# A GELU feed-forward kernel: the order of loads and transposes in its first six microseconds

## The chip, the core and the metric

The kernel runs on one core of one Trainium2 chip. The metric is the device time of one execution, in microseconds, as the median of several runs. Times inside an execution come from one profiled execution and are counted from the start of its span.

## What is computed

```python
B, S, D, F = 1, 2048, 448, 1792          # all bfloat16
def reference(x, w1, b1, w2, b2):
    h = jnp.einsum("bsd,df->bsf", x, w1) + b1
    h = _gelu(h)                          # tanh approximation
    return jnp.einsum("bsf,fd->bsd", h, w2) + b2
```

x is 2048 tokens by 448, w1 448 by 1792, w2 1792 by 448.

## The kernel before

Layer 1 computes the hidden activations transposed: an output tile has 128 hidden features on the partitions and 512 tokens (a chunk) along the free side. There are 4 chunks and 14 feature tiles, so 56 tiles, in the list `order`. Eight PSUM banks hold tiles in turn. ScalarE (ACT) applies Gelu with the bias b1 to each finished tile and writes it to `g_sb`. Layer 2 (`l2`) then takes 128 tokens at a time over the 14 feature tiles; VectorE (DVE) adds b2 and the SyncE queue (SP) stores the rows.

The contraction of layer 1 has length 448, cut into four slots of rows of w1 (`KROW`): three of 128 rows, and the remaining 64 rows held twice, so that two half-height passes can share the array. TensorE's work in layer 1 is the list `steps`: each step is two matmuls (passes), for tiles i and i+1. The first 23 steps are written out by hand in `OPEN`; a fourth number in an entry picks one half (256 tokens) of chunk 0. In the text, step 0 is `(0, 2, 0, 0)`: tiles 0 and 1, slot 0, first half of the tokens. Step 1 is the same for tiles 2 and 3. Steps 2 and 3 are these with the second half of the tokens; steps 4 and 5 are slot 0 of tiles 4 to 7, all 512 tokens; steps 6 and 7 slot 1 of tiles 0 to 3.

The matmuls need x with the contraction on the partitions. For chunks 1 to 3 DMA transposes do that (`load_xT`). Chunk 0 is loaded as it is, in two halves, into `xn_sb` (semaphores `sem_xn[0]` and `sem_xn[1]`), and TensorE turns it: `turn_x(n)` multiplies 128 by 128 blocks with an identity matrix that GpSimd (POOL) makes, and a cast brings the result from PSUM into `xT_sb`. The work is cut into six parts, each with the engine of its cast ("d" VectorE, "a" ScalarE) and its pairs (half, slot):

```python
    XPARTS = [
        ("d", [(0, 0)]), ("a", [(0, 1)]), ("a", [(0, 2), (0, 3)]),
        ("d", [(1, 0)]), ("d", [(1, 1)]), ("a", [(1, 2), (1, 3)]),
    ]
    XBANK = [0, 2, 4, 5, 6, 7]
```

Each pair is two transposes, so the six parts are 2, 2, 4, 2, 2 and 4. `XBANK` is the PSUM bank that a part's result stands in until it is cast; the tile of that number can't be begun before. Parts 0 to `XLATE` - 1 are turned before step 0, the others just before step `EARLY` = 2. Before the first transpose TensorE runs constant matmuls (`NWARM` of `WN` columns) whose results nobody reads. `opening_waits` makes a step wait for the pieces of w1 and the casts that its passes read: step 0 for w1's first piece (slot 0, tiles 0 to 3) and part 0; step 2 for part 3.

Loads are issued from two queues. SP (`sync_work`) issues x's two halves, then w1's pieces of slots 0 and 1 (`load_w1p`, four pieces of 128 KB in all, of which one is on ACT's queue), the rest of w1, the DMA transposes, w2 and b2. ACT (`scalar_work`) issues b1 and w1's first piece, then loads its function table and makes its casts.

Of the kernel before, what the change touches and what calls it, by code (L numbers as in the profile page):

```python
# [7 lines left out]
BF16 = mybir.dt.bfloat16  # L8
# [3 lines left out]
def bass_standalone__dense_activation_gelu__prompt_kernel(  # L12
# [10 lines left out]
    P = 128  # L23
# [18 lines left out]
    W1_PIECES = [(0, 4), (4, 8)]  # L42
# [26 lines left out]
    ]  # L69
    XBANK = [0, 2, 4, 5, 6, 7]  # L70

    XLATE = 5
    EARLY = 2

    SQ = 32
    NB = 8

    NWARM = 12
    WN = 256


    OCUT = 320
# [42 lines left out]
    with ExitStack() as es:  # L125
# [4 lines left out]
        xn_sb = sb("xn_sb", [P, STC, D], BF16)  # L130
# [8 lines left out]
        ps = [es.enter_context(nc.psum_tensor(f"ps_{i}", [P, SC], FP32)) for i in range(NB)]  # L139
# [9 lines left out]
        sem_xn = [S_(f"sem_xn{i}") for i in range(2)]  # L149
# [17 lines left out]
        x0_view = x2[0:SC, :].rearrange("(p t) d -> p t d", t=STC)  # L167
        out0_view = out2[0:SC, :].rearrange("(p t) d -> p t d", t=STC)

        def store(eng, n):  # L170
            j, c0, c1 = outs[n]
            to = out0_view[:, j, c0:c1] if j < STC else out2[j * P:(j + 1) * P, c0:c1]
            eng.dma_start(to, out_sb[:, j, c0:c1]).then_inc(sem_od, 16)

        def x_part(n, parts):
            h, k = parts[0]
            to = xT_sb[:, k:k + len(parts), 2 * h * P:2 * (h + 1) * P]
            src = ps[XBANK[n]][:, 0:2 * P * len(parts)]
            return to, src.rearrange("p (k t) -> p k t", k=len(parts))

        def load_w1p(eng, k, i):
            a, b = W1_PIECES[i]
            r = KROW[k]
            with nc.allow_non_contiguous_dma(reason="w1 column pieces"):
                eng.dma_start(
                    w1_sb[:, k, a * P:b * P], w1[r:r + P, a * P:b * P]
                ).then_inc(sem_w1p[k][i], 16)

        def load_w1(eng):
            with nc.allow_non_contiguous_dma(reason="w1 column pieces"):  # L190
                for k in (3, 2):
                    n, r = ROWS[k], KROW[k]
                    eng.dma_start(w1_sb[0:n, k, 0:WCUT], w1[r:r + n, 0:WCUT]).then_inc(sem_w1[k], 16)
                eng.dma_start(w1_sb[:, 3, WCUT:F], w1[KROW[3]:D, WCUT:F]).then_inc(sem_w13, 16)
                eng.dma_start(
                    w1_sb[:, 0:2, WCUT:F], w1[0:2 * P, WCUT:F].rearrange("(k p) f -> p k f", p=P)
                ).then_inc(sem_w1r, 16)
                eng.dma_start(
                    w1_sb[0:HALF, 2, WCUT:F], w1[KROW[2]:KROW[2] + HALF, WCUT:F]
                ).then_inc(sem_w1r, 16)  # L200

        def load_w2(eng, i):
            a, b = W2_PIECES[i]
            eng.dma_start(
                w2_sb[:, a:b, :], w2[a * P:b * P, :].rearrange("(ft p) d -> p ft d", p=P)
            ).then_inc(sem_w2[i], 16)

        def load_xT(eng, c):
            for k, d0 in enumerate(KROW):
                eng.dma_start(  # L210
                    xT_sb[:, k, c * SC:(c + 1) * SC],
                    x2[c * SC:(c + 1) * SC, d0:d0 + P],
                    transpose=True,
                ).then_inc(sem_x[c], 16)

        def sync_work(sp):
            sp.dma_start(xn_sb[:, 0:2, :], x0_view[:, 0:2, :]).then_inc(sem_xn[0], 16)
            sp.dma_start(xn_sb[:, 2:4, :], x0_view[:, 2:4, :]).then_inc(sem_xn[1], 16)
            load_w1p(sp, 0, 1)
            for i in range(len(W1_PIECES)):  # L220
                load_w1p(sp, 1, i)
            load_w1(sp)
            load_xT(sp, 1)
            for c in range(2, NSC):
                load_xT(sp, c)
            for i in range(len(W2_PIECES)):
                load_w2(sp, i)
            sp.dma_start(b2_bc[:, :], b2.partition_broadcast(P)).then_inc(sem_b2, 16)
            for n in range(len(outs) - 1):
                sp.wait_ge(sem_osb, n + 1)  # L230
                store(sp, n)
            sp.wait_ge(sem_od, 16 * len(outs))
# [10 lines left out]

        def tensor_work(pe):
            ones_w = nc.const_aps.tensor(1.0, [P, P], BF16)
            ones_x = nc.const_aps.tensor(1.0, [P, WN], BF16)
            for _i in range(NWARM):
                pe.matmul(ps[0][:, 0:WN], lhsT=ones_w, rhs=ones_x, start=True, stop=True)  # L248
            pe.wait_ge(sem_id, 2)

            def turn_x(n):
                parts = XPARTS[n][1]
                for h, k in parts:
                    if (h, k) in ((0, 0), (1, 0)):
                        pe.wait_ge(sem_xn[h], 16)
                    for t in range(2):
                        col = parts.index((h, k)) * 2 * P + t * P
                        mm = pe.matmul(  # L258
                            ps[XBANK[n]][:, col:col + P],
                            lhsT=xn_sb[:, 2 * h + t, KROW[k]:KROW[k] + P],  # L260
                            rhs=ident[:, :],
                            start=True, stop=True,
                        )
                mm.then_inc(sem_xtp, 1)
# [46 lines left out]
            def l1():  # L311
                for n, (i, h, m, tokens) in enumerate(steps):
                    if n == EARLY:
                        for x in range(XLATE, len(XPARTS)):
                            turn_x(x)
# [45 lines left out]

            for x in range(XLATE):
                turn_x(x)
# [3 lines left out]

        def scalar_work(act):
            act.dma_start(b1n_sb[0:NFT, :], b1.rearrange("(c p) -> c p", p=P)).then_inc(sem_b1n, 16)
            load_w1p(act, 0, 0)  # L370
            zero = nc.const_aps.tensor(0.0, [P, 8], FP32)
            act.activation(act_junk[:, :], zero, ACT.Gelu_apprx_tanh)  # L372
            for n, (e, parts) in enumerate(XPARTS):
                if e == "a":
                    act.wait_ge(sem_xtp, n + 1)
                    act.copy(*x_part(n, parts)).then_inc(sem_xTa, 1)  # L376
            act.wait_ge(sem_b1, 1)
            for i, (c, ft) in enumerate(order):
                act.wait_ge(sem_l1, i + 1)
                act.activation(  # L380
                    g_sb[:, ft, c * SC:(c + 1) * SC], bank("g", i)[:, :], ACT.Gelu_apprx_tanh,
                    bias=b1_f[:, ft:ft + 1], scale=1.0,
                ).then_inc(sem_g, 1)
            act.wait_ge(sem_osb, len(outs))
            store(act, len(outs) - 1)
# [26 lines left out]


        sync_work(nc.sync)
        gpsimd_work(nc.gpsimd)
        tensor_work(nc.tensor)
        scalar_work(nc.scalar)
        vector_work(nc.vector)

# [27 lines left out]
```

## Time and profile before

| | |
|---|---|
| median of 3 runs | 93.98 us (93.93 to 94.01) |
| profiled execution, its own time | 93.20 us |
| its span | 91.9 us |
| TensorE busy | 89.2 us (97%) |
| weight loads busy | 47.3 us (52%) |
| ScalarE busy | 36.6 us (40%) |
| VectorE busy | 12.8 us (14%) |
| granted TensorE clock, mean | 1.00 |
| layer 1 passes | 384 matmuls, 42.8 us |
| layer 2 | 238 matmuls, 42.6 us |
| constant matmuls | 12, 2.7 us |
| transposes of chunk 0 | 16, 1.6 us |

In the lines of the profile, PE is TensorE's matmuls and PEld its weight loads; `ps` is a PSUM bank, `xn_sb` x as loaded, `xT_sb` x turned, `wi_sb` w1, `wo_sb` w2. A line number such as L258 is that of the kernel: L248 the constant matmuls, L258 the transposes, L275 layer 1's passes, L354 layer 2, L376 the casts on ScalarE, L391 those on VectorE, L380 Gelu. A busy TensorE is not one at its peak: the matmuls are pipelined, and a short wait can be covered by the modelled end of the one before, so starts of matmuls are read rather than busy shares.

### The profile page before, as it was taken

The page shows a single profiled execution, that of the slowest core. Times are in us where ns is not written, and L with a number is a line of the kernel's source. Part 1 is how long each engine was busy: PE and PEld are TensorE (multiplying, and loading weights), DVE is VectorE, ACT ScalarE, POOL GpSimd, SP SyncE. Part 2 cuts the span into 40 slices and gives each one's busy share as a digit, 9 for nine tenths or more (in the row PEclk, how much of TensorE's full clock was granted, in tenths as well). Part 3 has the DMA queues.
Part 4 walks back from the last instruction along what each step waited for, and adds up shares of the span by engine and source line. Part 5 has one row for each costly group of instructions (what it writes and reads, how often), then busy time and mean ns, then how long its engine had stood idle before and what let it go on. Part 6 is the DMA issues. An engine that isn't in the chain of part 4 may idle for free.

```text
span 91.9 us, 1491 instructions
## 1 busy us (share of the span) xinstructions
PE 89.2 (97%) x650; PEld 47.3 (52%) x650; DVE 12.8 (14%) x27; ACT 36.6 (40%) x61; POOL 1.3 (1%) x7
## 2 busy tenths in 40 slices
PE   6999999999999999999999999999999999999991
PEld 4664445555555555555545555555555555555571
DVE  0172000000000000000000122222112222221141
ACT  2640999877977788778974000000000000000000
POOL 5000000000000000000000000000000000000000
PEclk9999999999999999999999999999999999999999
DMA  1999856445795000000000111011111100111111
GB/s 26 342 303 274 143 112 85 95 101 114 199 375 182 0 0 4 7 0 0 0 0 0 50 55 47 7 48 50 50 50 50 50 28 29 50 50 50 50 50 50
DMA packets 12594, 7.29 MB, mean 79 GB/s; under 512 B 7203, under 2 KB 12396, under 8 KB 12588
## 3 DMA queue, kind: packets, MB, share of 16 engines
q1 hardware_dynamic: 12240, 7.03, 29.1%
q10 hardware_dynamic: 316, 0.17, 0.6%
q8 instruction: 5, 0.08, 0.3%
q0 software_dynamic: 32, 0.00, 0.0%
q14 instruction: 1, 0.01, 0.0%
HBM read 3.79 MB, written 1.84 MB: 61 GB/s over the span
## 4 chain that ended last, share of the span: by engine, by line
PE 97%; DVE 0%; issue 0%
PE ps L275 46%; PE ps L354 46%; PE ps L248 3%; PE ps L258 2%; DVE out_sb L408 0%
## 5 line engine op out<-in xcount | busy, mean ns | idle before, releaser
L275 PE MATMUL ps<-xT_sb,wi_sb 64*128 64x512 bf16 (+2 forms) x384 | 42.8, 374 | 0.0
L354 PE MATMUL ps<-wo_sb,g_sb 128*128 128x448 bf16 (+2 forms) x238 | 42.6, 342 | 0.0
L380 ACT ACTIVATE g_sb<-ps,bi_f 128x512 bf16<-128x512 f32 x56 | 33.7, 694 | 9.5 <-PE ps L275 9.5
L354 PEld LDWEIGHTS ps<-wo_sb,g_sb 128*128 128x128 bf16 x238 | 22.7, 98 | 20.2 <-issue 0.4
L275 PEld LDWEIGHTS ps<-xT_sb,wi_sb 64*128 64x128 bf16 (+1 forms) x384 | 21.8, 94 | 20.4 <-issue 0.7
L408 DVE TENSOR_TENSOR out_sb<-ps,bo_bc 128x448 bf16<-128x448 f32 (+2 forms) x17 | 10.2, 597 | 71.2 <-PE ps L354 71.2
L248 PE MATMUL ps<-const-bfloat16-1.0 128*128 128x256 bf16 x12 | 2.7, 417 | 0.8 <-PEq L432 0.8
L248 PEld LDWEIGHTS ps<-const-bfloat16-1.0 128*128 128x128 bf16 x12 | 1.6, 143 | 1.4 <-issue 0.8
L372 ACT ACT_TABLE_LOAD x1 | 1.3, 1283 | 1.8 <-issue 1.8
L376 ACT CAST xT_sb<-ps 128x512 bf16<-128x512 f32 (+1 forms) x3 | 1.5, 514 | 1.3 <-PE ps L258 1.3
L391 DVE CAST xT_sb<-ps 128x256 bf16<-128x256 f32 x3 | 1.2, 422 | 4.2 <-PE ps L258 4.2
L258 PE MATMUL ps<-ident,xn_sb 128*128 128x128 bf16 x16 | 1.6, 251 | 0.0
L258 PEld LDWEIGHTS ps<-ident,xn_sb 128*128 128x128 bf16 x16 | 1.3, 116 | 0.6 <-issue 0.5
L404 DVE COPY wi_sb<-wi_sb 64x512 bf16<-64x512 bf16 (+1 forms) x2 | 0.6, 286 | 2.0 <-DMA wi_sb<-in_w_dram 2.0
L396 DVE STREAM_TRANSPOSE bit_sb<-bin_sb 32x32 bf16<-32x32 bf16 x4 | 0.8, 200 | 0.1
L242 POOL DMA_DIRECT2D bin_sb<-in_w_dram x1 | 0.7, 655 | 0.2 <-issue 0.2
L237 POOL TENSOR_SCALAR_AFFINE_SELECT ident<-ident 128x128 bf16<-128x128 bf16 x1 | 0.3, 287 | 0.2 <-POOL ident L235 0.2
L372 ACT ACTIVATE act_junk<-const-float32-0.0 128x8 bf16<-128x8 f32 x1 | 0.2, 208 | 0.0
L235 POOL MEMSET ident<- 128x128 bf16 x1 | 0.2, 204 | 0.3 <-POOLq L432 0.3
L398 DVE CAST bi_f<-bit_sb 128x14 f32<-128x14 bf16 x1 | 0.2, 175 | 0.0
L432 POOL MEMSET const-float32-0.0<- 128x1 f32 x1 | 0.1, 98 | 0.2 <-issue 0.2
L432 POOL MEMSET const-bfloat16-1.0<- 128x1 bf16 x1 | 0.1, 101 | 0.0
(2 smaller groups left out, 0.2 us busy)
## 6 DMA issues: line engine op xcount, KB each, us to landing
out_dram<-out_sb SPq DMA_DIRECT2D x15, 112.0 KB, 1.7
wo_sb<-in_w_dram SPq DMA_DIRECT2D x2, 784.0 KB, 5.5
wi_sb<-in_w_dram SPq DMA_DIRECT2D x4, 128.0 KB, 3.5
xn_sb<-in_x_dram SPq DMA_DIRECT2D x2, 224.0 KB, 2.8
wi_sb<-in_w_dram SPq DMA_DIRECT2D x1, 384.0 KB, 5.1
wi_sb<-in_w_dram SPq DMA_DIRECT2D x1, 256.0 KB, 4.0
wi_sb<-in_w_dram SPq DMA_DIRECT2D x1, 192.0 KB, 4.5
xT_sb<-in_x_dram SPq DMA_TRANSPOSE x12, 3.4
```

Of the source, the lines that this page charges most:

```text
L242: pool.dma_start(b1n_sb[NFT:SQ, :], w1[0:SQ - NFT, 0:P]).then_inc(sem_b1x, 16)
L248: pe.matmul(ps[0][:, 0:WN], lhsT=ones_w, rhs=ones_x, start=True, stop=True)
L258: mm = pe.matmul(ps[XBANK[n]][:, col:col + P], lhsT=xn_sb[:, 2 * h + t, KROW[k]:KROW[k] + P], rhs=ident[:, :], start=True, stop=True,)
L275: return pe.matmul(bank("g", i)[:, t0:t1], lhsT=w1_sb[lo:hi, k, ft * P:(ft + 1) * P], rhs=xT_sb[lo:hi, k, c * SC + t0:c * SC + t1], start= ...
L354: mm = pe.matmul(bank("o", n)[:, 0:c1 - c0], lhsT=g_sb[:, ft, j * P:(j + 1) * P], rhs=w2_sb[:, ft, c0:c1], start=(ft == 0), stop=(ft == NF ...
L372: act.activation(act_junk[:, :], zero, ACT.Gelu_apprx_tanh)
L376: act.copy(*x_part(n, parts)).then_inc(sem_xTa, 1)
L380: act.activation(g_sb[:, ft, c * SC:(c + 1) * SC], bank("g", i)[:, :], ACT.Gelu_apprx_tanh, bias=b1_f[:, ft:ft + 1], scale=1.0,).then_inc( ...
L391: dve.tensor_copy(*x_part(n, parts)).then_inc(sem_xTd, 1)
L396: dve.transpose(b1t_sb[to, :], b1n_sb[:, to]).then_inc(sem_b1T, 1)
L404: dve.tensor_copy(two(HALF, 2), two(0, 3)).then_inc(sem_dup, 1)
L408: dve.tensor_tensor(out=out_sb[:, j, c0:c1], in0=bank("o", n)[:, 0:c1 - c0], in1=b2_bc[:, c0:c1], op=ALU.add,).then_inc(sem_osb, 1)
```

## The change

Three things are changed in the opening, and nothing behind it. The order of x's and w1's first loads: SP issues x's first half and then w1's first piece; x's second half goes from SP to ACT, in the place where w1's first piece was. `XLATE` goes from 5 to 3: before step 0 only the first half of x is turned (8 transposes in place of 12), and the whole second half (8 in place of 4) behind steps 0 and 1, which are four passes of 256 columns. And three constant matmuls of 128 columns follow the twelve of 256.

```diff
-    XLATE = 5
+    XLATE = 3
     EARLY = 2
...
-    NWARM = 12
-    WN = 256
+    WARM = [256] * 12 + [128] * 3
...
         def sync_work(sp):
             sp.dma_start(xn_sb[:, 0:2, :], x0_view[:, 0:2, :]).then_inc(sem_xn[0], 16)
-            sp.dma_start(xn_sb[:, 2:4, :], x0_view[:, 2:4, :]).then_inc(sem_xn[1], 16)
-            load_w1p(sp, 0, 1)
+            for i in range(len(W1_PIECES)):
+                load_w1p(sp, 0, i)
             for i in range(len(W1_PIECES)):
                 load_w1p(sp, 1, i)
...
         def tensor_work(pe):
             ones_w = nc.const_aps.tensor(1.0, [P, P], BF16)
-            ones_x = nc.const_aps.tensor(1.0, [P, WN], BF16)
-            for _i in range(NWARM):
-                pe.matmul(ps[0][:, 0:WN], lhsT=ones_w, rhs=ones_x, start=True, stop=True)
+            for n in WARM:
+                ones_x = nc.const_aps.tensor(1.0, [P, n], BF16)
+                pe.matmul(ps[0][:, 0:n], lhsT=ones_w, rhs=ones_x, start=True, stop=True)
             pe.wait_ge(sem_id, 2)
...
             act.dma_start(b1n_sb[0:NFT, :], b1.rearrange("(c p) -> c p", p=P)).then_inc(sem_b1n, 16)
-            load_w1p(act, 0, 0)
+            act.dma_start(xn_sb[:, 2:4, :], x0_view[:, 2:4, :]).then_inc(sem_xn[1], 16)
```

## The prediction

> **What bounds the kernel now.** I read the page first, then the chain that ended last, then the opening's timeline, then the times to landing.
>
> ```profile
> span 91.9 us, 1491 instructions
> PE 89.2 (97%) x650; PEld 47.3 (52%) x650; DVE 12.8 (14%) x27; ACT 36.6 (40%) x61; POOL 1.3 (1%) x7
> ...
> PE 97%; DVE 0%; issue 0%
> ```
>
> TensorE is the bound from 0.79 us to 90.02. The chain of waits cut into pieces (start, length, what) says where:
>
> ```profile
> 0.79 2.72 PE ps L248 x12
> ...
> 3.52 1.17 PE ps L258 x12
> 4.69 0.56 PE ps L275 x4
> 5.25 0.22 PE ps L258 x4
> 5.48 42.02 PE ps L275 x380
> 47.49 42.53 PE ps L354 x238
> ```
>
> The change touches only what stands ahead of 5.48. Behind it lie 84.5 us of matmuls. So the question is one number: when does the third step of the opening (step 2: tiles 0 and 1, second half of the tokens) start, and does the rest move with it? The timeline of the opening, in start, length, what (first matmul of a group):
>
> ```profile
> 1.20 0.42 SPq L218 DMA_DIRECT2D xn_sb<-in_x_dram  x1
> 1.44 0.36 ACTq L185 DMA_DIRECT2D wi_sb<-in_w_dram  x1
> 3.52 1.17 PE L258 MATMUL ps<-ident,xn_sb 128*128 128x128 bf16 x12
> 3.93 0.42 DVE L391 CAST xT_sb<-ps 128x256 bf16<-128x256 f32 x1 [3.93 <-PE ps L258]
> 4.62 0.76 DVE L391 CAST xT_sb<-ps 128x256 bf16<-128x256 f32 x2 [0.26 <-PE ps L258]
> 4.64 0.61 PE L275 MATMUL ps<-xT_sb,wi_sb 128*128 128x256 bf16 x4
> 5.09 0.39 PE L258 MATMUL ps<-ident,xn_sb 128*128 128x128 bf16 x4
> 5.31 8.94 PE L275 MATMUL ps<-xT_sb,wi_sb 128*128 128x256 bf16 x72
> ```
>
> and, from the DMA issues, KB and us to landing:
>
> ```profile
> xn_sb<-in_x_dram SPq DMA_DIRECT2D x2, 224.0 KB, 2.8
> wi_sb<-in_w_dram ACTq DMA_DIRECT2D x1, 128.0 KB, 3.2
> ```
>
> The second line is w1's first piece: issued at 1.44, landed at 4.64 by these rounded numbers, and step 0's first matmul starts at 4.64. Its other input, the first cast, had ended at 3.93 + 0.42 = 4.35. So steps 0 and 1 wait for w1 and not for x. Taken singly, the x loads land 2.6 and 3.0 us after issue: first half 0.75 + 2.6 = 3.35, second 1.20 + 3.0 = 4.2. From 4.64 to 5.31 TensorE is full: four passes to 5.09, four transposes to 5.31. The second half's first cast (part 3) began at 4.62 and was done near 5.0, before step 2 wanted it at 5.31: it costs nothing now.
>
> **The change, part by part.**
>
> Three constant matmuls of 128 columns. The twelve of 256 columns start from 0.79 to 3.08, 0.21 each at the end, so the last leaves the array at 3.08 + 0.21 = 3.30. TensorE then waits for x until 3.52. Three of half the width take 3 x 0.107 = 0.32 and end at 3.62. Of the 0.32, 0.22 fill the wait and 0.10 is pushed onto the transposes: the first goes from 3.52 to 3.62. In the trace the second follows at 3.58 (its weights were there), the third at 3.68, a pitch of 0.107; without the pause I take that pitch for all, so the second goes from 3.58 to 3.73: +0.15. At the least the constants cost nothing (if x lands later than 3.5), at the most 0.15.
>
> w1's first piece on SP's queue, second place. It goes out at 1.20 and not 1.44. The 224 KB transfer that held this place landed 3.0 after issue, at 4.25 at the latest; the next SP pieces took 3.2 and 3.3, which would give 4.5. I take 4.2, as less is ahead of it. It is wanted when the first cast is done, which comes out at 4.50 below, so at either end it is hidden. SP has as many issues ahead of every later load as it had, so nothing else on SP moves.
>
> The first cast and step 0. The cast of part 0 begins 3.93 - 3.58 = 0.35 after the second transpose starts. After: 3.73 + 0.35 = 4.08, plus 0.425 for the cast is 4.50, plus 0.04 from a release to the next engine's start (the transposes of part 0 end at 3.58 + 0.31 = 3.89, the cast starts at 3.93) is 4.55 with the digits that rounding drops. Step 0 moves from 4.64 to 4.55: **-0.09**. That is all the earlier piece brings, because the first cast takes w1's place as the last input.
>
> x's second half on ACT's queue. The issue takes 0.42 where w1's took 0.36; ACT sits idle for 0.8 us before its first cast, so that costs nothing. The data go out at 1.44 instead of 1.20. By the row of the ACT issue it lands 3.2 later, at 4.64; at the least at 4.25 as before. At the most it waits for the two w1 pieces that follow on SP; the second of these (issued 2.13, 3.2 to landing) lands at 5.35. It is wanted after the four passes, at 4.55 + 0.45 = 5.00, so I take 4.64 and no cost; 5.35 would add 0.40.
>
> [...]
>
> The second half is turned behind four passes. In the kernel before, four of its eight transposes ran before 4.53, under the wait for w1, and the other four at 5.09; now all eight stand behind step 1. Four more transposes on the path, at 0.055 each (warm: 0.22 for the four at 5.09): **+0.22**. They end at 4.55 + 0.45 + 0.44 = 5.44. But step 2 needs part 3's cast, and that now begins only after the passes: its second transpose starts at 5.00 + 0.055 = 5.05, takes 0.22 to its end, 0.04 to VectorE (0.26 in all), 0.425 for the cast, 0.04 back: 5.05 + 0.26 + 0.425 + 0.04 = 5.78. TensorE stands idle from 5.44 to 5.78: **+0.33**. The cover that is gone is steps 0 and 1, which lay between part 3's transposes and its use.
>
> Who waits behind it: everything on TensorE from step 2 on, in order. Part 4's cast on VectorE follows part 3's (5.73 to about 6.15); its bank is first wanted by tile 6 at 5.78 + 0.44 + 0.43 = 6.65. Part 5's on ACT begins near 5.65 and ends by 6.24; tile 7 wants it at 6.86. b1's conversions end at about 7.3 instead of 6.39, and the first Gelu starts no earlier than 9.36. All covered. Nothing after 5.8 gives time back: w1's pieces are there earlier than they are used, and the one visible hole, 0.31 between matmul starts at 7.26 and 7.57 instead of 0.216, stands again as 0.31 between 47.12 and 47.42, both where the passes change between half and whole rows; I read it as that change's cost. If the first were a wait, 0.10 would be taken up there.
>
> Sum: -0.09 + 0.22 + 0.33 = **+0.46 us**: step 2 from 5.31 to 5.78, rounded. Against the profiled execution (93.20, its span 91.9 and 1.3 around it) that is a span of 92.36 and 93.66. The median of the runs is 0.78 above the profiled time; nothing in the trace places that difference, so I carry the 0.46 over: 93.98 + 0.46 = **94.44**. With the constants free (+0.37) or the hole a wait (+0.36) it is 94.35; with both 94.25.
>
> **The rivals.** A difference under 0.2% (0.19 us) can't be told from no change here.
>
> The clock flips later. In the trace the transposes' pitch falls from 0.107 to 0.056 near 4.15, some 3.4 after the first constant. Suppose it comes after 6.3 in the timed runs. Then before: the twelfth transpose starts at 3.58 + 10 x 0.107 = 4.65, step 0 at 4.76, four passes of 0.213 to 5.61, four transposes to 6.04. After: step 0 still at 4.55, passes to 5.40, part 3's second transpose at 5.51, 0.35 and 0.425 and 0.04 on, 6.33. That is 0.29 at half clock, 0.15 of full work: 94.13, no measurable change. Against it: 2.2 us more of half clock cost 1.1, more than the 0.78 by which the timed runs lie above the profile. Chance 0.07.
>
> [...]
>
> Faster: the constants bring the clock forward. [...] Chance 0.11.
>
> x's second half lands late, from 5.00 on, up to 5.35: 94.44 to 94.84. [...] Against: in the trace w1's first piece, in the very same place, took 3.2. Chance 0.12.
>
> That the change doesn't do what it says is ruled out by the two instruction orders: eight transposes, four 256-column passes, eight transposes, as described.
>
> **How the numbers follow.** Forecast 0.70 (94.25 to 94.55), late half 0.12, late clock 0.07, earlier clock 0.11. The range takes in the late clock at the bottom and half of the late-landing case at the top: 94.10 to 94.65. Faster 0.11, same 0.07, slower 0.82.
>
> **What would show it.** In the profile after: the first transpose at 3.62; step 0 at 4.55, released by VectorE's cast and not by w1; eight transposes in one group behind four passes; VectorE's second cast at about 5.31; an idle weight load of some 0.33 before step 2, at 5.78; span 92.36. Step 2 before 5.5, or a hole of under 0.1 there, proves me wrong in the mechanism; a start past 5.9 points at the late half of x.

## The result and the profile after

Over 22 runs of each kernel, the changed kernel's median is 94.03 us (93.57 to 94.33) and that of the kernel before 93.48 us (93.09 to 94.20). The ratio of their times is put at 1.0041 with a 95% interval of 1.0022 to 1.0060: slower by 0.38 us, between 0.2 and 0.56. It isn't the quotient of the two medians, which are 0.55 apart; the means are 0.43 apart. So the loss is clear, and its size in the timed runs is known to a few tenths only. The three runs of before that stood at the head of this document, 93.93 to 94.01, are among the 22 and lie near their top: only three of the other 19 reach 93.93. In the experiments, one of the twelve runs of the kernel with the new order of loads alone took 95.75 us, apart from all others, and its ratio leaves that run out.

The page after, and the chain that ended last, cut into pieces in order of time (start, length, what; the lines of the kernel are one further down, so L259 are the transposes, L276 layer 1's passes, L392 VectorE's casts):

```profile
span 92.8 us, 1497 instructions
PE 90.0 (97%) x653; PEld 48.2 (52%) x653; DVE 12.8 (14%) x27; ACT 36.7 (40%) x61; POOL 1.3 (1%) x7
```

```profile
4.68 0.93 PE ps L276 x4
5.61 0.12 PE ps L259 x2
...
5.76 0.44 DVE xT_sb L392
...
6.24 42.19 PE ps L276 x380
48.43 42.53 PE ps L355 x238
```

VectorE has come into the chain: the cast of part 3 now stands between two pieces of TensorE's work. Step 2 starts at 6.24, before at 5.31. Everything behind it has its old length (42.5 us for layer 2 in both), so the spans differ by what the opening lost, 0.93. The timeline shows what that consists of (its lines of TensorE's matmuls and VectorE's casts, and the weight loads ahead of step 2):

```profile
3.62 1.06 PE L259 MATMUL ps<-ident,xn_sb 128*128 128x128 bf16 x8
4.08 0.42 DVE L392 CAST xT_sb<-ps 128x256 bf16<-128x256 f32 x1 [4.08 <-PE ps L259]
4.65 0.96 PE L276 MATMUL ps<-xT_sb,wi_sb 128*128 128x256 bf16 x4
5.45 0.61 PE L259 MATMUL ps<-ident,xn_sb 128*128 128x128 bf16 x8
5.76 0.76 DVE L392 CAST xT_sb<-ps 128x256 bf16<-128x256 f32 x2 [1.26 <-PE ps L259]
6.24 1.84 PEld L276 LDWEIGHTS ps<-xT_sb,wi_sb 128*128 128x128 bf16 x12 [0.35 <-DVE xT_sb L392]
6.24 3.96 PE L276 MATMUL ps<-xT_sb,wi_sb 128*128 128x256 bf16 x26 [0.18 <-DVE xT_sb L392]
```

The four passes take from 4.65 to 5.45, 0.80; before, the same four took from 4.64 to 5.09, 0.45. They ran at half clock: their starts are up to 0.213 apart, where before they were 0.109 apart. The row of the granted clock reads 1.00 in this stretch of both profiles, so the moment at which the clock comes up (the flip) is read from the spacing of the starts; in an experiment below whose row does show 0.50, the passes stand 0.213 apart too. In this execution the flip came near 5.4, in the profile of before near 4.15. So 0.35 of the 0.93 is the clock's. From 5.45 to 6.24 it is 0.79, where before the stretch from the last pass to step 2 was 0.22: that 0.57 is the change's, with 0.22 for the four more transposes and 0.35 for which the weight loads stand idle until VectorE's cast is done. (The 0.18 in PE's own line is shorter because it counts from the modelled end of the last transpose.) Step 0 itself has not moved (4.64, 4.65). Two profiles thus give a loss of 0.93, the timed runs of 0.38, and the sum of the prediction 0.46; the experiments are to say which part belongs to the change.

### The profile page after: what moved, and what is told of

It is laid out like the page before. It is cut to its first block, busy times and chain, and to the rows that moved or that the text cites. A ratio compares the mean times of both kernels' runs of the same rounds, so it can differ in the third digit from the quotient of the medians.

```text
span 92.8 us, 1497 instructions
## 1 busy us (share of the span) xinstructions
PE 90.0 (97%) x653; PEld 48.2 (52%) x653; DVE 12.8 (14%) x27; ACT 36.7 (40%) x61; POOL 1.3 (1%) x7
## 4 chain that ended last, share of the span: by engine, by line
PE 97%; DVE 1%; issue 0%
PE ps L276 46%; PE ps L355 46%; PE ps L249 3%; PE ps L259 1%; DVE xT_sb L392 0%; DVE out_sb L409 0%
## 5 line engine op out<-in xcount | busy, mean ns | idle before, releaser
L276 PE MATMUL ps<-xT_sb,wi_sb 64*128 64x512 bf16 (+2 forms) x384 | 43.2, 376 | 0.2 <-DVE xT_sb L392 0.2
L276 PEld LDWEIGHTS ps<-xT_sb,wi_sb 64*128 64x128 bf16 (+1 forms) x384 | 22.0, 94 | 20.8 <-issue 0.9
L249 PE MATMUL ps<-const-bfloat16-1.0 128*128 128x256 bf16 (+1 forms) x15 | 3.0, 397 | 0.8 <-PEq L433 0.8
L249 PEld LDWEIGHTS ps<-const-bfloat16-1.0 128*128 128x128 bf16 x15 | 2.1, 146 | 1.5 <-issue 0.8
L392 DVE CAST xT_sb<-ps 128x256 bf16<-128x256 f32 x3 | 1.2, 422 | 5.3 <-PE ps L259 5.3
L259 PE MATMUL ps<-ident,xn_sb 128*128 128x128 bf16 x16 | 1.7, 267 | 0.0
L259 PEld LDWEIGHTS ps<-ident,xn_sb 128*128 128x128 bf16 x16 | 1.5, 128 | 0.1
```

What stands on the lines that cost most here:

```text
L249: pe.matmul(ps[0][:, 0:n], lhsT=ones_w, rhs=ones_x, start=True, stop=True)
L259: mm = pe.matmul(ps[XBANK[n]][:, col:col + P], lhsT=xn_sb[:, 2 * h + t, KROW[k]:KROW[k] + P], rhs=ident[:, :], start=True, stop=True,)
L276: return pe.matmul(bank("g", i)[:, t0:t1], lhsT=w1_sb[lo:hi, k, ft * P:(ft + 1) * P], rhs=xT_sb[lo:hi, k, c * SC + t0:c * SC + t1], start= ...
L392: dve.tensor_copy(*x_part(n, parts)).then_inc(sem_xTd, 1)
```

## The experiments

Two theories. **Cover**: the loss is the four more transposes on the path and the cast of part 3, which lost steps 0 and 1 as its cover; the clock comes up at its own time, whatever the kernel does. **Clock**: the change itself, by its constants, moved the clock's flip from 4.1 to 5.4. The timed results, each against runs of before taken beside it (step 0 and step 2 from the one profiled execution). The first row's fastest run belongs to the four kernels in the middle; the fastest of before beside the changed kernel is 93.09, beside the last row 93.10.

| kernel | ratio, 95% interval | fastest run | step 0 | step 2 |
|---|---|---|---|---|
| before | 1 | 93.06 | 4.64 | 5.31 |
| changed | 1.0041 (1.0022 to 1.0060) | 93.57 | 4.65 | 6.24 |
| constants only | 1.0001 (0.9972 to 1.0030) | 93.06 | 4.65 | 5.30 |
| change without constants | 1.0036 (1.0004 to 1.0067) | 93.49 | 4.46 | 6.20 |
| loads only | 1.0048 (1.0014 to 1.0081) | 93.35 | 4.80 | 5.46 |
| turn late only | 1.0044 (1.0015 to 1.0073) | 93.61 | 4.79 | 6.03 |
| turn behind two passes | 1.0036 (1.0005 to 1.0067) | 93.49 | 4.65 | 6.18 |

**The constants alone.**

```diff
-    NWARM = 12
-    WN = 256
+    WARM = [256] * 12 + [128] * 3
```

> The kernel before with nothing but the three constant matmuls of 128 columns added. Cover theory (the loss is the four more transposes and the cast of part 3 that lost its cover; the clock flips when it will, whatever the kernel does): 0.00 to +0.10 us against before; step 2 between 5.31 (flip near 4.1) and 6.2 (flip after 6). Clock theory (the three constants move the flip from 4.1 to about 5.4, as in the two profiles at hand): half of 1.3 us, +0.5 to +0.65 us, and a flip near 5.4 again. If the constants bring the clock forward: -0.3 us or less.

The ratio is 1.0001, and the profile (timeline of TensorE) shows passes at full clock from the start, so the clock was up by 4.65:

```profile
4.65 0.60 PE L274 MATMUL ps<-xT_sb,wi_sb 128*128 128x256 bf16 x4
5.08 0.39 PE L257 MATMUL ps<-ident,xn_sb 128*128 128x128 bf16 x4
5.30 1.46 PE L274 MATMUL ps<-xT_sb,wi_sb 128*128 128x256 bf16 x8
```

The interval, -0.26 to +0.28 us, holds neither the +0.5 of the clock theory nor the -0.3 expected if the constants bring the clock forward. That is the end of both.

**The change without the constants.**

```diff
-    WARM = [256] * 12 + [128] * 3
+    WARM = [256] * 12
```

> The changed kernel without the three constants. Cover theory: +0.44 us where the clock flips early, +0.07 where late, +0.25 to +0.4 in the mean, hardly less than the whole change (the constants cost under 0.1). Clock theory: the flip is back near 4.1 and the time within 0.1 us of before plus what the cover costs less the clock's 0.6, so -0.2 to 0.0.

1.0036: the loss stays. In its profile the clock was late as well (step 2 at 6.20, the flip just ahead of 6), without the three added constants to blame:

```profile
4.46 1.01 PE L276 MATMUL ps<-xT_sb,wi_sb 128*128 128x256 bf16 x4
5.26 0.93 PE L259 MATMUL ps<-ident,xn_sb 128*128 128x128 bf16 x8
```

One thing did move: step 0 starts at 4.46 and not at 4.65. So w1's earlier landing brings step 0 forward by 0.18 against the kernel before, and in the changed kernel the three constants, which push the first transposes from 3.48 to 3.62, take that back. What this is worth in the timed runs, 1.0036 and 1.0041 with these intervals can't tell.

**Only the second half turned late.**

```diff
-    XLATE = 5
+    XLATE = 3
```

> Only the second half of x is turned behind steps 0 and 1; loads and constants as before. Cover theory: step 0 still waits for w1 (4.65), step 2 at 5.87 with an early flip; +0.56 us there, +0.17 with a late one, +0.35 to +0.5 in the mean: as much as the whole change or a little more. Clock theory: the same transposes and no constants, so no change of the clock: under +0.2 us.

1.0044, so this one line costs as much as the whole change, within the intervals. Its timeline has the clock up early, so the loss stands there alone:

```profile
4.79 0.61 PE L275 MATMUL ps<-xT_sb,wi_sb 128*128 128x256 bf16 x4 [0.41 <-DMA wi_sb<-in_w_dram]
5.24 0.61 PE L258 MATMUL ps<-ident,xn_sb 128*128 128x128 bf16 x8
6.03 0.83 PE L275 MATMUL ps<-xT_sb,wi_sb 128*128 128x256 bf16 x5 [0.18 <-DVE xT_sb L391]
```

Step 0 waits for w1, in this execution until 4.79. From the first transpose behind the passes to step 2 it is 6.03 - 5.24 = 0.79, the same as in the changed kernel, and the wait is put down to VectorE's cast.

**Only the loads.**

```diff
-            sp.dma_start(xn_sb[:, 2:4, :], x0_view[:, 2:4, :]).then_inc(sem_xn[1], 16)
-            load_w1p(sp, 0, 1)
+            for i in range(len(W1_PIECES)):
+                load_w1p(sp, 0, i)
...
-            load_w1p(act, 0, 0)
+            act.dma_start(xn_sb[:, 2:4, :], x0_view[:, 2:4, :]).then_inc(sem_xn[1], 16)
```

> Only the order of the loads is changed (w1's first piece second on SP, x's second half on ACT); 12 transposes still stand before step 0, no constants added. Cover theory: step 0 now waits for x's second half (landing near 4.6) and the four transposes behind it, so step 0 at 4.85 to 5.06 and step 2 at 5.51 with an early flip; +0.10 to +0.20 us. Clock theory: no pause is closed, so the flip stays near 4.1, and +0.2 us.

The place of the loss is as expected: the four transposes ahead of step 0 wait for x's second half.

```profile
4.57 0.40 PE L259 MATMUL ps<-ident,xn_sb 128*128 128x128 bf16 x4 [0.26 <-DMA xn_sb<-in_x_dram]
```

Its size is not: step 2 comes at 5.46, 0.15 late, but the runs say 0.45, with an interval from 0.13 to 0.75. The lower end meets the expectation, the middle doesn't. A second half of x that lands later in other executions, as was seen once further down, would do it; that was not shown for this kernel, and its loss stays in part unexplained.

**The second half turned behind two passes.**

```diff
-    EARLY = 2
+    EARLY = 1
```

> The changed kernel with the second half of x turned behind step 0 (two passes) and not behind step 1 (four): step 1's passes then lie between part 3's transposes and its use and are cover again. Cover theory: step 2 at 5.63 with an early flip (changed kernel: 5.8), 6.25 with a late one (6.33); against before +0.3 us early, +0.05 to +0.1 late, +0.15 in the mean, about half of the change's loss. If part 3's cast is not what step 2 waits for, the time stays that of the changed kernel, +0.4 us.

1.0036, with an interval from 0.05 to 0.63 us: it holds both the 0.15 expected and the whole change, so it tells nothing between them. The profile fell on a late clock, where theory and rival differ by little in time (step 2 at 6.18). What the profile does show is that the wait is gone: step 1's two passes start at 5.88 and 6.07 and step 2 follows at 6.18, with no wait for VectorE ahead of it. Whether that pays with an early clock was not measured.

**Both kernels at a settled clock, first try.**

```diff
-    NWARM = 12
+    NWARM = 52
...
             pe.wait_ge(sem_id, 2)
+            pe.wait_ge(sem_w1r, 32)
```

> The kernel before with 52 constant matmuls in place of 12, and its first transpose waits for the last piece of w1 (landing near 10.3), so that clock and loads are settled before the opening begins. Cover theory: step 2 comes 1.45 us after the first transpose (12 transposes, cast of part 0, four passes, four transposes); the runs spread far less than the 1.1 us of before, under 0.5 (only the landing is left); some 6.5 us longer than before. If the spread of before's runs is not the clock's, it stays 1 us.

> The changed kernel with the same two alterations. Cover theory: step 2 comes 2.0 us after the first transpose, so it is 0.56 us slower than the kernel before altered in the same way, with nothing of clock or landing in the difference. If the loss came from the clock or from x's later landing, the two differ by the four transposes at most, under 0.25 us.

This failed as a pair: the runs spread over 2.0 us (99.59 to 101.63) and not under 0.5. The windows of the kernel before so altered (each with its length, the busy time of TensorE, weight loads, VectorE, ScalarE and GpSimd, then the granted clock, DMA share and GB/s) say why:

```profile
9.00:10.00 1.00, 0.00 (x0) 0.00 (x0) 0.00 (x0) 0.00 (x0) 0.00 (x0) 1.00 1.06 74
10.80:11.20 0.40, 0.40 (x5) 0.40 (x6) 0.00 (x0) 0.00 (x0) 0.00 (x0) 0.50 1.28 267
```

The constants ran out early, TensorE paused for 2.54 us, and its clock was halved (0.50) when the transposes began. In the changed kernel's profile the pause was 1.03 us and the clock stayed up; there step 2 came 2.11 after the first transpose. The single runs can be sorted by their mean granted clock. Where it is 1.00, the kernel before took 99.59, 99.77 and 100.41 and the changed one 100.21 and 100.31, with medians 0.49 apart. Where it is 0.983, they took 101.25 to 101.63 (three) and 101.44 to 101.87 (four), with medians 0.06 apart. So few runs are a sign and no proof, but they fit a loss that is there at full clock and nearly gone at half.

**Both kernels at a settled clock, with 64 constants.**

```diff
-    NWARM = 52
+    NWARM = 64
```

> As the kernel before with 52 constants and the wait for w1's last piece, but with 64 constants: TensorE then pauses about 1 us and not 2.5 us ahead of the first transpose, and keeps its full clock. Cover theory: from the first transpose to step 2 1.45 to 1.55 us, four transposes in 0.22, no wait ahead of step 2. If the long pause was not what halved the clock there, the interval is 2.5 us again.

> The changed kernel altered in the same way. Cover theory: from the first transpose to step 2 2.0 to 2.1 us, 0.56 more than the kernel before with 64 constants, of it 0.22 the four transposes and 0.33 the wait for VectorE's second cast. If the loss were the clock's or the loads', under 0.25 more.

The kernel before, and then the changed one:

```profile
10.55 0.83 PE L259 MATMUL ps<-ident,xn_sb 128*128 128x128 bf16 x12 [1.08 <-issue]
11.43 0.60 PE L276 MATMUL ps<-xT_sb,wi_sb 128*128 128x256 bf16 x4
12.09 2.11 PE L276 MATMUL ps<-xT_sb,wi_sb 128*128 128x256 bf16 x10
```

```profile
10.63 0.61 PE L260 MATMUL ps<-ident,xn_sb 128*128 128x128 bf16 x8
11.51 0.60 PE L277 MATMUL ps<-xT_sb,wi_sb 128*128 128x256 bf16 x4 [0.28 <-DVE xT_sb L393]
11.94 0.61 PE L260 MATMUL ps<-ident,xn_sb 128*128 128x128 bf16 x8
12.74 1.47 PE L277 MATMUL ps<-xT_sb,wi_sb 128*128 128x256 bf16 x7 [0.18 <-DVE xT_sb L393]
```

With everything landed and the clock full, step 2 comes 1.54 after the first transpose in the one and 2.11 in the other. The late turn costs **0.57 us**, as expected to 0.01, and nothing of it is a load or the clock; the three constants of 128 columns are not part of this pair. The two spans, 98.7 and 99.3, differ by that and by the 0.08 by which the first transpose starts later. Each of the two is one execution; the changed kernel with 52 constants had the same 2.11.

**The unchanged kernels once more.**

> The kernel before unchanged, for another phase of the clock. [...]

> The kernel before unchanged, a third phase of the clock: step 2 at 5.31 for a flip near 4.1, 5.56 for 5.0, 5.75 for 5.4, 6.05 for 6 and later.

> The changed kernel unchanged, for another phase of the clock. If the flip is independent of the kernel: step 2 at 5.80 with a flip near 4.1, 6.0 for 5.0, 6.2 for 5.4, 6.33 for 6 and later, and the span moves by about half of the flip's move. If the change sets the flip: 5.4 and 6.24 again.

The kernel before, second profile:

```profile
3.48 1.44 PE L258 MATMUL ps<-ident,xn_sb 128*128 128x128 bf16 x12
4.71 0.80 PE L275 MATMUL ps<-xT_sb,wi_sb 128*128 128x256 bf16 x4
...
5.57 1.25 PE L275 MATMUL ps<-xT_sb,wi_sb 128*128 128x256 bf16 x7
```

Twelve transposes at half clock (0.107 apart) end at 4.71, behind w1's landing (3.1 us after its issue); the clock comes up near 5.1 and step 2 starts at 5.57. The third profile has its flip near 5.0 and step 2 at 5.48, 0.08 ahead of the 5.56 expected for that flip. So the same kernel has spans of 91.9, 92.2 and 92.4. The last of these holds a further wait, after step 2, that held TensorE up in this profile and not in the first (weight loads, by whom they waited for; us, times, longest):

```profile
PEld ps L275 <- DMA wi_sb<-in_w_dram: 0.6, 1, 0.6
```

Here the piece of w1 with rows 256 to 319 landed 4.9 us after issue, where the first profile had 3.9; two matmuls stand 0.49 apart at 7.97 instead of 0.21.

The changed kernel's second profile had the clock up near 4.5, ahead of step 0, and another wait:

```profile
4.64 0.60 PE L276 MATMUL ps<-xT_sb,wi_sb 128*128 128x256 bf16 x4
5.28 0.62 PE L259 MATMUL ps<-ident,xn_sb 128*128 128x128 bf16 x8
6.08 0.83 PE L276 MATMUL ps<-xT_sb,wi_sb 128*128 128x256 bf16 x5 [0.18 <-DVE xT_sb L392]
```

The passes end at 4.64 + 0.44 = 5.08, but the transposes start at 5.28: x's second half landed 3.8 us after its issue at 1.44. Without that 0.20, step 2 would stand at 5.88. With the early flip of the first profile of before, 5.31 against 5.88 is again 0.57. The span, 92.7, is less than 0.2 below that of the first profile, and not half of the flip's move (0.5) as expected; the late half of x takes 0.20 of the difference.

Is the flip independent of the kernel? In the pair with 52 constants, and again in that with 64, TensorE runs the same constant matmuls in both kernels until the flip, and it came near 3.9 and 6.0 in the one pair and near 3.7 and 6.4 in the other. So a flip can move by more than two microseconds with nothing changed in TensorE's work. But in the seven profiles in which part 3 is turned ahead of step 0 the flip lies between 3.7 and 5.1, and in the seven in which it is turned later between 4.2 and 6.4. Whether that leaning is chance, so few profiles can't show.

## Why the prediction was right and wrong

**Right: direction, place and mechanism.** The eight transposes stand in one group behind four passes, VectorE's cast is what step 2 waits for, and nothing behind gives time back (the hole where passes change from whole to half rows is 0.31 in the profiles before and after). The term for the four transposes and the idle time for the cast, 0.22 + 0.33 = 0.55, measured 0.57 with the clock settled; the idle weight load forecast at 0.33 is 0.35 in the profile after. One of the prediction's signs misled, though: step 2 past 5.9 was to point at the late half of x. It came at 6.24, but that half had landed at 4.59, before the passes ended; the late start was the clock's.

**Mis-sized: step 0's -0.09.** It came out as zero: the first cast ends at 4.08 + 0.425 = 4.50, but step 0 starts at 4.65. I had put 0.04 on the way from cast to matmul, taken from a case in the other direction (transpose to cast). At step 0 it was 0.15 wherever the cast was the last to come: in both profiles of the changed kernel, in that without the three constants, and in both with 64 constants. So in the changed kernel w1's earlier landing (2.6 us after its issue at 1.21) brought nothing, because the cast, pushed back by the constants, came too late to use it, and the sum at full clock is 0.57 and not 0.46. Without the constants step 0 stood at 4.46, which would leave 0.39 (-0.18 + 0.22 + 0.35); the prediction had +0.37 for that case, without its working.

**Wrong: carrying the sum to the median.** The step "the median of the runs is 0.78 above the profiled time; nothing in the trace places that difference, so I carry the 0.46 over" failed, and with it the range 94.10 to 94.65, below which 94.03 lies by 0.07. The 0.78 was neither a constant nor a property of the timed runs: before's runs go from 93.06 to 94.31, the profiled execution was one with an early clock, and three runs that happened to lie at 93.9 to 94.0 were taken as the level. With the median of 22 in place of that of three, the 0.78 is 0.28. From 93.48 the same sum gives 93.94, and with the 0.57 measured 94.05. That the forecast missed by no more than 0.41 is in part luck: the level was 0.50 too high, and the sum about 0.1 too low.

**Wrong: how little the late clock was given.** I gave 0.07 to the clock's flip coming later in the timed runs, with the one flip of one profile to go by. The flip moves between executions of one program: near 4.15, 5.0 and 5.1 in three profiles of the kernel before and near 4.5 and 5.4 in two of the changed one. The consequence that this rival worked out shows at the slow end of the runs only: the fastest ones differ by 0.48 (93.09 and 93.57), the medians by 0.55, the slowest by 0.13 (94.20 and 94.33), where the rival's half-clock estimate gave 0.15. This fits a loss of 0.57 that shrinks when the clock is very late, because TensorE at half clock has work to do while the cast runs: in the changed kernel without the constants the eight transposes last 0.93 us, to 6.19, with no wait on TensorE ahead of step 2 at 6.20, where at full clock they last 0.61 and step 2 waits for the cast. That the average is made up in this way was not measured run by run. The late piece of w1, for which weight loads of the kernel before waited 0.6 us in its third profile and those of the changed kernel not at all in its first, takes a share that I can't size. No run shows the constants bringing the clock forward, which was given 0.11: alone they have the ratio 1.0001, and step 2 at 5.30.

**The late half of x.** It was given 0.12. x's second half, on ACT's queue, landed at 4.59 and 5.23 in two profiles of the changed kernel; it cost nothing in the first and 0.20 in the second. Over seven profiles each, it landed 3.1 to 3.8 us after issue on ACT's queue and 2.9 to 3.1 as second on SP's; what makes the difference is not shown here.

**No version beats the kernel before.** Each part was undone or done alone: the constants are free in the kernel before, the late turn loses, and the new order of loads loses where the second half is turned early. Not tried were the new loads without the constants together with the turn behind two passes.

## What to carry to other kernels

An operand that is produced in a chain of engines (transpose, cast, matmul) must be begun a whole chain ahead of its use; when its start is moved, ask first what lay between start and use, since that cover is lost even if no work is added. Before adding a difference to a measured time, find out how widely single runs spread and at which end of that spread the profiled one lies; three runs that agree need not be the level. When several inputs gate a step, making one earlier is worth only the distance to the next.

## What was not expected of the hardware

TensorE's clock fell to 0.50 after a pause of 2.54 us in one execution and stayed at 1.00 after pauses of 1.03 and 1.08 us in two others. The clock's flip in the opening moved by about a microsecond between executions of the same program (near 4.15 and 5.1 in the kernel before, near 4.5 and 5.4 in the changed one); the two spans of the kernel before are 91.9 and 92.2. And from the end of a cast to step 0, which waits for cast and w1 both, it took 0.15 us, nearly three times what the last wait of step 2 took (VectorE's cast ends at 5.76 + 0.425 = 6.185, step 2 starts at 6.24). Whether the second wait is the reason was not tested.
